# New costs, hand-overs and a table of ranks for the planner of a fused attention and mixture-of-experts kernel

## The chip, the cores and the metric

The kernel runs on one core of a Trainium2 chip. The metric is the time of one execution on the device in microseconds; the time shown is the median of three runs. The core has five engines that each run their own list of instructions in order and hand over by semaphores: PE (matrix products; its weight loads are listed as PEld), DVE, ACT, POOL and SP, which issues the transfers. Operands lie in an on-chip memory of 128 partitions; products accumulate in eight banks beside it.

## The reference

Inputs: `q`, `k`, `v` of shape (8, 8, 576, 64): 8 batches of 8 heads with 576 positions of 64 numbers; `phi` of shape (8, 8, 576, 32); a routing matrix `moe_phi` (512, 32) and the weights `w1` (8, 512, 1024) and `w2` (8, 1024, 512) of 8 experts. All is float32.

```python
def _attn_ref(q, k, v, phi):
    a = softmax(phi over the 576 positions)
    k_m = einsum('bhsm,bhsd->bhmd', a, k)     # 32 pooled keys
    v_m = einsum('bhsm,bhsd->bhmd', a, v)     # 32 pooled values
    attn = softmax(scale * q @ k_m^T over the 32)
    return attn @ v_m

def _moe_ref(x, phi, w1, w2):                 # x: (4608, 512)
    logits = x @ phi                          # (4608, 32 slots)
    d = softmax(logits over the 4608 rows)
    slot_input = d.T @ x                      # 4 slots per expert
    slot_out[e] = relu(slot_input[e] @ w1[e]) @ w2[e]
    c = softmax(logits over the 32 slots)
    return c @ slot_out
```

The softmaxes are shortened here: subtract the maximum, take the exponential, divide by the sum plus 1e-9. The softmax over 4608 rows spans all batches, so no expert can start before the last batch has been routed.

## The kernel before

**Stages.** The 8 batches are worked in four pairs (`bp` 0 to 3, `g` 0 and 1 within a pair). For a batch, `pool_phi` loads `phi` (576 KB), takes its maximum (DVE, line 541, then a transpose and products on PE, lines 549 and 563), subtracts it (POOL, 579), takes the exponential (ACT, 585), and sums by a tree of additions (POOL, 592) and a product with a mask (PE, 602). `pool_kv` loads `k` and `v` (1152 KB each), pools them in three groups of products (PE, 629), scales the sums (ACT, 645 and 652), turns them (PE, 665 and 670), copies them (ACT, 675 to `vT` and 684 to `kd`), and makes products with `moe_phi` (PE, 692) that are copied to `vpb` (ACT, 705). `q` (1152 KB) is loaded into one of two buffers of the tensor `top` and transposed in two halves (DVE, 730). Then, for a pair and each of four chunks `c` of heads: scores (PE, 746), a transpose (DVE, 760), a softmax over the 32 pooled keys (DVE 776, POOL 781, ACT 786, DVE 791 and 800, POOL 804), a transpose back (DVE, 807) and the slot logits (PE, 815). `route` (from `weigh` on, lines 833 to 1032) takes the exponentials of the logits, the products of these with the attention weights (PE, 943), two more groups of products (979 and 987, and 1018), and stores what the pair adds to the slots' input. For the last pair it ends in SIM, the slots' input (DVE, line 1127).

**Experts and output.** From SIM on PE multiplies with `w1` (line 1227) and `w2` (line 1278), 16 tiles of 1 MB each, the last tile of `w2` loaded in four pieces. Then come the slots' sums (1204, 1211), rounding in two parts (1394, 1399), the output products (1408), copies (1461, 1463) and the stores.

**Space.** Nearly all buffers lie in one tensor, `arena`. 20 buffers for weight tiles lie over those of attention; two more weight tiles go where `q` lay. A weight tile can be loaded when the attention buffers below it have been used for the last time. Four of the 20 have nothing below them. Two buffers each serve `phi` and the pairs of `k` and `v`.

**The order.** The class `Plan` writes the order out. Each step is registered by `add(engine, cost, function, reads, writes, ...)`, with a cost in microseconds and a rank. `order` keeps a time for each engine and for the transfers, and repeatedly takes the step that can start first: its inputs are done, plus a lag (0.2 us, 0.25 if the reader is PE, 0 on the same engine), its engine is free and buffers for its results are free. Ties go to the lower rank. A load's start is the time at which the transfers are free; it ends after its bytes at 380 GB/s plus 2 us. The steps are then issued in this order, so every engine runs its part of it as a fixed list, whatever the real times are. SP's list of loads is one of them: a load whose buffer isn't free holds up the loads behind it. Ranks are set by `plan.at(x)`: 1000 x, growing from step to step. Before, they follow a formula in the pair's number, among them `bp - 1.15 + 0.5 * g` for pooling, `bp - 0.45` for the loads of `q`, `bp + 0.25 * c` for chunks and `bp + 1.2` for routing; weights and all that follows have 20. The first nine loads have a fixed order (`FIRST`). Costs come from short formulas for each engine; that for PE is

```python
def pe(n, cols, cnt, passes=2, tiles=1):
    return n * max(0.0185, (cols / 1200.0 + cnt * passes / 2400.0) / tiles)
```

`fill` adds products with a matrix of ones (line 506), 40 of them registered for the start at the lowest rank, and ten around the last pair's routing. Those for the start are left out where the plan's time is past 25 us.

Of the kernel before, what the change touches and what calls it, by code (L numbers as in the profile page):

```python
# [20 lines left out]
class Plan:  # L21
# [7 lines left out]
    LAG = 0.2  # L29
    LAG_PE = 0.25  # L30
# [3 lines left out]
    FILL_END = 25.0  # L34

# [9 lines left out]
    def add(self, eng, cost, fn, r=(), w=(), also=(), pri=None, dma=0.0, slack=0.0):  # L45
        i = len(self.ops)
# [28 lines left out]
        self.ops.append((eng, cost, fn, deps, pri, dma, tiles, need, slack))  # L75

    def order(self):
# [10 lines left out]
        dma_free = 0.0  # L88
        out = []
        while ready:  # L90
# [28 lines left out]
            eng, cost, _, _, pri, dma, tiles, need, _ = ops[i]  # L119
# [13 lines left out]
            for x in tiles:  # L133
                x.users -= 1
                x.end = max(x.end, end[i] + self.LAG)
# [121 lines left out]
def kernel(  # L257
# [174 lines left out]
    WC = 0.45  # L432
# [23 lines left out]
    add(DVE, 1.8, f, r=[ident_b], w=[maskhp_b, maskc_b, rep_b, ones_b])  # L456
# [27 lines left out]
    DMA_RATE = 380e3  # L484

    def load(dst, src, nbytes, w, pri=None):
        add(
            SP, 0.06, lambda: nc.sync.dma_start(dst(), src), w=[w],
            dma=nbytes / DMA_RATE, pri=pri,
        )  # L490


    FIRST = ["phi0", "phi1", "mphi", "q0", "k0", "v0", "q1", "k1", "v1"]
# [30 lines left out]
    add(POOL, 1.0, f, r=[mphi_b], w=[mphd_b])  # L524
# [6 lines left out]
    def pool_phi(b):  # L531
        pt = phis.tile()
        ph = lambda: pt.ap.rearrange("p (c j m) -> p c j m", c=C, j=J)
        load(
            lambda: pt.ap.rearrange("p (c x) -> p c x", c=C), rows(phi, b), H * S * M * 4, pt,
            pri=first(f"phi{b}"),
        )
        mx, mh, mb, es, rs = pmxs.tile(), pmhs.tile(), pmbs.tile(), pess.tile(), prss.tile()
        add(
            DVE, 2.2,  # L540
            lambda: nc.vector.tensor_reduce(  # L541
                mx.ap, ph().rearrange("p c j m -> p c m j"), axis=AX.X, op=ALU.max
            ),
            r=[pt], w=[mx],
        )
        t0 = b_m.tile()
        add(
            PE, TP,
            lambda: nc.tensor.transpose(t0.ap[:, :P], mx.ap.rearrange("p c m -> p (c m)"), ident),
            r=[mx, ident_b], w=[t0], also=[mh],  # L550
        )
        add(
            DVE, dve(P),
            lambda: nc.vector.tensor_reduce(
                mh.ap, t0.ap[:, :P].rearrange("x (a p) -> x a p", a=2), axis=AX.X, op=ALU.max
            ),
            r=[t0], w=[mh],
        )
        t1 = b_m.tile()

        def f():
            for a in range(2):
                nc.tensor.matmul(
                    t1.ap[HALF * a: HALF * a + HALF, :P],
                    mh.ap[:, a: a + 1].to_broadcast([P, HALF]),
                    ident,
                    start=True,
                    stop=True,
                )

        add(PE, pe(4, HALF, P, tiles=2), f, r=[mh, ident_b], w=[t1], also=[mb])
        add(
            ACT, act(128),
            lambda: nc.scalar.copy(mb.ap.rearrange("p c m -> p (c m)"), t1.ap[:, :P]),  # L574
            r=[t1], w=[mb],
        )
        add(
            POOL, pool_tt(PHI_SZ),
            lambda: nc.gpsimd.tensor_tensor(  # L579
                ph(), ph(), mb.ap.unsqueeze(2).to_broadcast([P, C, J, M]), op=ALU.subtract  # L580
            ),
            r=[mb, pt], w=[pt],
        )
        add(
            ACT, act(PHI_SZ, False), lambda: nc.scalar.activation(pt.ap, pt.ap, AF.Exp),  # L585
            r=[pt], w=[pt],
        )
        tr = trees.tile()

        def f():  # L590
            t = tr.ap
            plus = lambda o, x, y: nc.gpsimd.tensor_tensor(o, x, y, op=ALU.add)  # L592
            plus(t, ph()[:, :, 0:4, :], ph()[:, :, 4:8, :])
            plus(t[:, :, 0:2], t[:, :, 0:2], t[:, :, 2:4])
            plus(t[:, :, 0], t[:, :, 0], t[:, :, 1])
            plus(es.ap, t[:, :, 0], ph()[:, :, 8, :])

        add(POOL, pool_tt(512) + pool_tt(256) + 2 * pool_tt(128), f, r=[pt], w=[es, tr])
        sp = b_m.tile()
        add(  # L600
            PE, pe(2, 128, 2),
            lambda: nc.tensor.matmul(
                sp.ap[:, :2], es.ap.rearrange("p c m -> p (c m)"), maskhp, start=True, stop=True
            ),
            r=[es, maskhp_b], w=[sp], also=[rs], slack=S_SLACK,
        )

        def f():
            nc.vector.tensor_scalar(rs.ap, sp.ap[:, :2], EPS, None, op0=ALU.add)
            nc.vector.reciprocal(rs.ap, rs.ap)  # L610

        add(DVE, 0.32, f, r=[sp], w=[rs])
        return pt, ph, rs

    def pool_kv(b, pt, ph, rs, vpb):

        kb = kvs.tile().split(2)
        kv = lambda: kb.ap.rearrange("p (i c x) -> p i c x", i=2, c=C)
        for i, (src, name) in enumerate(((k, "k"), (v, "v"))):
            load(lambda i=i: kv()[:, i], rows(src, b), H * S * D * 4, kb.part(i), pri=first(f"{name}{b}"))  # L620
        acc = b_kv.tile()
        kp, vm = kps.tile(), vms.tile()

        def f(js):
            for j in js:
                for c in range(C):
                    for a in range(2):
                        h0 = HALF * a
                        nc.tensor.matmul(  # L629
                            acc.ap[M * c: M * c + M, a, : 2 * D],  # L630
                            ph()[h0: h0 + HALF, c, j, :],
                            kv()[h0: h0 + HALF, :, c, j * D: j * D + D],
                            start=(j == 0),
                            stop=(j == J - 1),
                            tile_position=(h0, M * c),
                        )

        for js in (range(0, 3), range(3, 6), range(6, 9)):
            add(
                PE, pe(2 * len(js) * H, M, 2 * D, tiles=8), lambda f=f, js=js: f(js),  # L640
                r=[pt, kb], w=[acc], also=[kp, vm],
            )
        def f():
            for a in range(2):
                nc.scalar.activation(
                    kp.ap.rearrange("p i (r x) -> p i r x", r=R)[:, :, :, HALF * a: HALF * a + Y],
                    acc.ap[:, a, :D].rearrange("p (i x) -> p i x", i=2).unsqueeze(2)
                    .to_broadcast([P, 2, R, Y]),
                    AF.Copy, scale=rs.ap[:, a: a + 1],
                )  # L650
            for a in range(2):
                nc.scalar.activation(  # L652
                    vm.ap[:, a], acc.ap[:, a, D: 2 * D], AF.Copy, scale=rs.ap[:, a: a + 1]
                )

        add(ACT, 2 * act(P) + 2 * act(D), f, r=[acc, rs], w=[kp, vm])

        tp, tv = b_m.tile(), b_m.tile()
        kd, vT = kbs.tile(), vTs.tile()

        def f():
            o = tp.ap.rearrange("p (i c r m) -> p i c r m", i=2, c=C, r=R)
            for i in range(2):
                for r in range(R):
                    nc.tensor.transpose(o[:, i, :, r, :], kp.ap[:, i, r * P: r * P + P], ident)

        add(PE, 4 * 0.11, f, r=[kp, ident_b], w=[tp], also=[kd])
        add(
            PE, TP,
            lambda: nc.tensor.transpose(tv.ap[:, :P], vm.ap.rearrange("p a d -> p (a d)"), ident),  # L670
            r=[vm, ident_b], w=[tv], also=[vT],
        )
        add(
            ACT, act(2 * P),
            lambda: nc.scalar.copy(
                vT.ap,
                tv.ap[:, :P].rearrange("p (c m) -> p c m", c=C).unsqueeze(2)
                .to_broadcast([P, C, R, M]),
# [829 lines left out]
```

## Time and profile before

| | |
|---|---|
| median of 3 runs (lowest to highest) | 209.78 us (209.73 to 210.0) |
| the profiled execution | 209.3 us, with a span of 207.5 us |
| mean granted clock of PE | 0.931 |
| busy, of the span: PE, DVE, POOL, ACT | 82%, 64%, 41%, 34% |
| read, written | 66.65 MB, 9.44 MB |
| SIM written, last expert product begun | 145.68 us, 177.34 us |
| waits of SP for PE's pooled products (line 629) | 39.5 us in 7 waits |
| waits of SP for DVE's reciprocal (line 800) | 15.5 us in 3 waits |

The span runs from the first to the last instruction; the time of the execution includes what lies around it. Times in the trace count from the start of the span. A row of a group gives line, engine, operation, result and input, count, then busy time and the mean of one in ns, then the time for which the engine stood idle before it and who ended the wait. "issue" there means that the trace shows nothing that was waited for. The DMA share is the mean busy share of the 16 transfer engines and can come out slightly above 1. A busy PE is not a PE at full speed: its clock is granted in steps, and the column for it is 1.00 at full clock.

### The profile page before, as it was taken

To read this page: it belongs to the slowest core of one execution; us is meant where nothing else is said; L and a number is where in the kernel's file an instruction comes from. 1 tells how busy PE (TensorE), PEld (TensorE's weight loads), DVE (VectorE), ACT (ScalarE), POOL (GpSimd) and SP (SyncE) were. 2 spreads that over 40 slices of the span, in tenths; PEclk is the share of its full clock that TensorE was granted. 3 is DMA by queue.
4 is the path that set the end of the run, shared out by engine and by line. 5 is a ranking of instruction groups with operands and counts; after the bars stand their busy time and mean duration, and the time that the engine had idled before them with its cause. 6 is when DMAs were issued, how large, how long until landed. Compare 5 with 4: busy or idle time off the path is not lost.

```text
span 207.5 us, 5943 instructions
## 1 busy us (share of the span) xinstructions
PE 170.3 (82%) x2571; PEld 109.1 (53%) x2571; DVE 133.3 (64%) x232; ACT 69.8 (34%) x183; POOL 84.4 (41%) x84
## 2 busy tenths in 40 slices
PE   7899777788299899769997979699999999999400
PEld 6577654546176466437566535456556555646100
DVE  7843244969916999995797499547609580387600
ACT  2031425246341661531664233211001331466400
POOL 7199107779690489389793248400000000000000
PEclk9999999969859999996999699999999999999855
DMA  6999999999999999999988999999999998079996
GB/s 207 367 391 393 381 389 381 390 382 384 390 380 392 387 391 406 345 393 390 378 325 288 400 411 417 405 409 407 400 413 405 412 405 302 2 292 410 417 417 287
DMA packets 28986, 76.47 MB, mean 369 GB/s; under 512 B 1824, under 2 KB 6944, under 8 KB 28960
## 3 DMA queue, kind: packets, MB, share of 16 engines
q1 hardware_dynamic: 28960, 76.09, 96.4%
q8 instruction: 20, 0.33, 0.7%
q14 instruction: 6, 0.05, 0.1%
HBM read 66.65 MB, written 9.44 MB: 367 GB/s over the span
## 4 chain that ended last, share of the span: by engine, by line
PE 50%; DVE 16%; DMA 14%; POOL 6%; issue 4%; ACT 2%; SPq 1%; DVEq 1%; POOLq 0%; ACTq 0%
DMA top<-in_q_dram 11%; PE bank L1227 7%; PE bank L815 6%; PE scbank L746 6%; PE kvbank L629 5%; PE kvbank L506 5%; PE kvbank L1278 4%; DMA out_dram<-arena 4%; PE scbank L1278 3%; DVE arena L730 3%; PE bank L1408 3%; PE bank L943 2%; POOL arena L804 2%; DVE arena L760 2%; DVE arena L541 2%
## 5 line engine op out<-in xcount | busy, mean ns | idle before, releaser
L579 POOL TENSOR_TENSOR arena<-arena 128x1152 f32<-128x1152 f32 x8 | 21.0, 2630 | 16.2 <-ACT arena L574 13.6
L506 PE MATMUL kvbank<-ones 128*128 128x256 f32 x88 | 25.2, 421 | 2.2 <-ACT arena L652 1.1
L730 DVE STREAM_TRANSPOSE arena<-top 128x1152 f32<-128x1152 f32 x16 | 21.7, 1360 | 7.2 <-DMA top<-in_q_dram 7.2
L815 PE MATMUL bank<-arena 128*128 128x288 f32 x64 | 21.7, 467 | 4.7 <-DVE arena L807 4.7
L746 PE MATMUL scbank<-arena 64*64 64x288 f32 x256 | 22.0, 442 | 3.0 <-DVE arena L760 2.5
L804 POOL TENSOR_TENSOR arena<-arena,ssm 128x576 f32<-128x576 f32 x16 | 18.3, 1152 | 15.0 <-DVE ssm L800 15.0
L592 POOL TENSOR_TENSOR arena<-arena 128x128 f32<-128x128 f32 (+2 forms) x32 | 23.4, 730 | 2.3 <-ACT arena L585 0.3
L781 POOL TENSOR_TENSOR arena<-arena,smx 128x576 f32<-128x576 f32 x16 | 18.4, 1152 | 13.6 <-DVE smx L776 13.6
L629 PE MATMUL kvbank<-arena 64*32 64x128 f32 x1152 | 21.6, 286 | 2.4 <-issue 1.8
L629 PEld LDWEIGHTS kvbank<-arena 64*32 64x32 f32 x1152 | 17.2, 110 | 6.5 <-issue 4.3
L506 PEld LDWEIGHTS kvbank<-ones 128*128 128x128 f32 x88 | 16.8, 205 | 6.9 <-issue 2.1
L541 DVE TENSOR_REDUCE arena<-arena 128x128 f32<-128x1152 f32 x8 | 17.1, 2142 | 3.9 <-DMA arena<-in_phi_dram 3.9
L760 DVE STREAM_TRANSPOSE arena<-scbank 128x576 f32<-128x576 f32 x16 | 12.2, 764 | 9.3 <-PE scbank L746 9.3
L815 PEld LDWEIGHTS bank<-arena 128*128 128x128 f32 x64 | 12.0, 207 | 10.8 <-DVE arena L807 6.4
L1408 PE MATMUL bank<-sr,cT 64*128 64x512 f32 (+1 forms) x78 | 14.2, 420 | 1.4 <-DVE arena L1463 0.8
L746 PEld LDWEIGHTS scbank<-arena 64*64 64x64 f32 x256 | 9.5, 142 | 11.0 <-DVE arena L760 4.5
L807 DVE STREAM_TRANSPOSE arena<-arena 128x576 f32<-128x576 f32 x16 | 12.2, 760 | 4.0 <-POOL arena L804 3.9
L786 ACT ACTIVATE arena<-arena 128x576 f32<-128x576 f32 x16 | 11.0, 688 | 8.5 <-POOL arena L781 8.5
L1463 DVE COPY arena<-bank 128x512 f32<-128x512 f32 x17 | 11.0, 687 | 3.7 <-DMA out_dram<-arena 2.4
L1227 PE MATMUL bank<-arena,SIM 128*32 128x256 f32 x224 | 12.5, 379 | 0.4 <-DVE SIM L1127 0.4
L1408 PEld LDWEIGHTS bank<-sr,cT 64*128 64x128 f32 x78 | 8.3, 184 | 7.3 <-DVE arena L1463 5.3
L776 DVE TENSOR_REDUCE smx<-arena 128x18 f32<-128x576 f32 x16 | 11.8, 738 | 0.3
(130 smaller groups left out, 242.4 us busy)
## 6 DMA issues: line engine op xcount, KB each, us to landing
arena<-in_moe_w_dram SPq DMA_DIRECT2D x29, 1024.0 KB, 10.1
top<-in_q_dram SPq DMA_DIRECT2D x8, 1152.0 KB, 13.6
arena<-in_k_dram SPq DMA_DIRECT2D x8, 1152.0 KB, 10.7
arena<-in_v_dram SPq DMA_DIRECT2D x8, 1152.0 KB, 13.1
out_dram<-arena SPq DMA_DIRECT2D x11, 768.0 KB, 8.2
arena<-in_phi_dram SPq DMA_DIRECT2D x8, 576.0 KB, 8.1
top<-in_moe_w_dram SPq DMA_DIRECT2D x2, 1024.0 KB, 6.3
arena<-in_moe_w_dram SPq DMA_DIRECT2D x4, 256.0 KB, 14.7
```

The lines of the kernel that those rows point to most:

```text
L506: lambda: nc.tensor.matmul(warm.ap, ones, ones.unsqueeze(1).to_broadcast([P, 2, P]), start=True, stop=True,),
L541: lambda: nc.vector.tensor_reduce(mx.ap, ph().rearrange("p c j m -> p c m j"), axis=AX.X, op=ALU.max),
L579: lambda: nc.gpsimd.tensor_tensor(ph(), ph(), mb.ap.unsqueeze(2).to_broadcast([P, C, J, M]), op=ALU.subtract),
L592: plus = lambda o, x, y: nc.gpsimd.tensor_tensor(o, x, y, op=ALU.add)
L629: nc.tensor.matmul(acc.ap[M * c: M * c + M, a, : 2 * D], ph()[h0: h0 + HALF, c, j, :], kv()[h0: h0 + HALF, :, c, j * D: j * D + D], start= ...
L730: nc.vector.transpose(qT.ap.rearrange("p (i u y) -> p u i y", i=2, y=Y), qt.ap[:, h * QT_SZ: h * QT_SZ + QT_SZ].rearrange("p (u i x) -> p ...
L746: nc.tensor.matmul(scb.ap[HALF * g: HALF * g + HALF, a, :JY], kb[g].ap[h0: h0 + HALF, i, c].rearrange("p r m -> p (r m)"), qT[g][c // 2].a ...
L781: lambda: nc.gpsimd.tensor_tensor(exv(), exv(), bc(mx), op=ALU.subtract),
L804: lambda: nc.gpsimd.tensor_tensor(exv(), exv(), bc(sm), op=ALU.mult),
L815: nc.tensor.matmul(lp.ap[:, :JY], vpb.ap[:, h, :], aT.ap[:, a * JY: (a + 1) * JY], start=(h == 0), stop=(h == H - 1),)
L1227: nc.tensor.matmul(hb.ap[NS * j: NS * j + NS, :256], SIM.ap[:, 2 * i + c, NS * e: NS * e + NS], wv[:, c, 256 * j: 256 * j + 256], start=(e ...
L1408: nc.tensor.matmul(po.ap[:, : x.stop - x.start], cT[bp].ap[y: y + HALF, j // 2 * P: j // 2 * P + P], sr.ap[y: y + HALF, t, x], start=(t == 0),
```

## The change

The planner's model is changed. The lag is now counted by the engine that hands over: 0.25 us for PE, 0.07 for DVE, ACT and POOL, 0 for SP. Transfers start at 2.3 us; attention's inputs are planned at 386 GB/s and weights at 412. For PE each step has a number of instructions, and the plan lets it cross a block of 256 of them no sooner than 6 us after the crossing before. Some costs are replaced by others.

The steps of a batch are regrouped into a class `Batch` with the parts `load_phi`, `shifted`, `load_kv`, `summed`, `pooled`, `turned`, `load_q` and `turn_q`. It could cut a batch into two units (`HALVES`), but that tuple is empty, so all batches have one. The computation and the shapes of instructions are those of before; in `turned` the copy to `kd` is registered ahead of that to `vT`. Each part has a rank of its own, read from a table with a row for the first pair, the two middle pairs and the last pair.

```diff
-    LAG = 0.2
-    LAG_PE = 0.25
+    LAG = (0.25, 0.07, 0.07, 0.07, 0.0)
+    BLOCK, BLOCK_US, FIRST_BLOCK = 256, 6.0, 193
+    DMA_START = 2.3
...
+        cost, ni = cost if isinstance(cost, tuple) else (cost, 4)
...
+            elif eng == PE:
+                for _ in range(ni):
+                    count += 1
+                    if count == self.BLOCK:
+                        count = 0
+                        x = t + cost / 2
+                        late = max(0.0, crossed + self.BLOCK_US - x)
+                        cost += late
+                        crossed = x + late
...
-                        r = max(r, end[d] + (0.0 if same else self.LAG_PE if ops[u][0] == PE else self.LAG))
+                        r = max(r, end[d] + (0.0 if same else self.LAG[ops[d][0]]))
...
-    WC = 0.45
+    WC = 0.49
...
-    add(DVE, 1.8, f, r=[ident_b], w=[maskhp_b, maskc_b, rep_b, ones_b])
+    add(DVE, 3.0, f, r=[ident_b], w=[maskhp_b, maskc_b, rep_b, ones_b])
...
-    DMA_RATE = 380e3
+    DMA_RATE = 412e3
+    IN_RATE = 386e3
...
-    add(POOL, 1.0, f, r=[mphi_b], w=[mphd_b])
+    add(POOL, 3.6, f, r=[mphi_b], w=[mphd_b])
...
-        add(POOL, pool_tt(512) + pool_tt(256) + 2 * pool_tt(128), f, r=[pt], w=[es, tr])
+            add(POOL, 0.5 + 2.66 / self.units, f, r=[pt.part(u)], w=[es.part(u), tr])
...
-                PE, pe(2 * len(js) * H, M, 2 * D, tiles=8), lambda f=f, js=js: f(js),
+                    PE, (0.075 * len(js) * self.ks, 8 * len(js) * self.ks), lambda f=f, js=js: f(js),
...
-        add(PE, 4 * 0.11, f, r=[kp, ident_b], w=[tp], also=[kd])
+            add(PE, (0.5, 8), f, r=[kp.part(u), ident_b], w=[tp], also=[kd])
...
-        add(PE, 0.4, f, r=[vT, mphd_b], w=[vpp], also=[vpb])
+            add(PE, (0.13 * ks, 4 * ks), f, r=[vT.part(u), mphd_b], w=[vpp], also=[vpb])
...
-        add(PE, 1.0, f, r=[qT[0][c // 2], qT[1][c // 2], *kb], w=[scb], also=[ex])
+        add(PE, (1.05, 32), f, r=[*(x.qT[c // 2] for x in pair), *(x.kd.part(x.part(c)) for x in pair)], w=[scb], also=[ex])
...
-        add(PE, 0.96, f, r=[aT, vpb], w=[lp])
+        add(PE, (1.1, 8), f, r=[aT, *(vpb.part(4 * u + x) for x in range(4))], w=[lp])
...
-        add(PE, 1.3 if bp < NSEG - 1 else 1.65, f, r=[df, ex], w=wp, also=[wt])
+        add(PE, (1.6, 72), f, r=[df, ex], w=wp, also=[wt])
...
-        add(PE, 1.3, f, r=[wt, rep_b], w=[wtp], also=[wtb])
+        add(PE, (1.4, 24), f, r=[wt, rep_b], w=[wtp], also=[wtb])
...
-        add(PE, 0.6, f, r=[wtb, *vm], w=[sip])
+        add(PE, (0.5, 16), f, r=[wtb, *(x.vm for x in pair)], w=[sip])
...
+    HALVES = ()
+    AT = (
+        dict(
+            phi=(-1.705, -2.946, -2.863, -1.886), kv=(-0.702, -0.388, -0.807, 0.687),
+            pool=(-1.466, -0.339, -1.36, -1.856), q=(-2.516, -1.841, -2.166, -2.025),
+            turn=(0.504, -0.618), chunk=(0.032, 0.327, 0.478, 0.492),
+            logit=(1.313, -0.355, -1.3, 0.485), route=-0.034,
+        ),
+        dict(
+            phi=(-3.631, -2.992), kv=(-1.771, -2.348), pool=(-0.774, -0.615), q=(0.409, 1.558),
+            turn=(1.059, 0.998), chunk=(0.106, 0.219, 0.401, 0.611),
+            logit=(-2.612, -2.214, -1.572, -0.776), route=1.408,
+        ),
+        dict(
+            phi=(-0.872, -0.956), kv=(-0.757, -0.522), pool=(-1.049, -0.412), q=(-1.042, -1.118),
+            turn=(-0.279, 0.997), chunk=(0.501, 0.524, -0.903, 1.688),
+            logit=(-0.899, 0.078, -1.255, 0.253), route=1.446,
+        ),
+    )
...
-            plan.at(bp - 1.15 + 0.5 * g, 8)
...
-        plan.at(bp - 0.45)
...
-            plan.at(bp - 0.2 + 0.4 * h)
...
-            plan.at(bp + 0.25 * c, 15)
...
-        plan.at(bp + (1.2 if bp < NBP - 1 else 1.0), 10)
+        units = 2 if bp in HALVES else 1
+        vpb = vpbs.tile().split(4 * units)
+        pair = [Batch(2 * bp + g, units) for g in range(2)]
+        at = AT[(bp > 0) + (bp == NBP - 1)]
+        for u in range(units):
+            for x in pair:
+                i = 2 * u + x.g
+                plan.at(bp + at["phi"][i], 8)
+                x.load_phi(u)
+                x.shifted(u)
+                plan.at(bp + at["kv"][i], 8)
+                x.load_kv(u)
+                plan.at(bp + at["pool"][i], 8)
+                x.summed(u)
+                x.pooled(u)
+                x.turned(u, vpb)
+            for x in pair:
+                plan.at(bp + at["q"][2 * u + x.g])
+                x.load_q(u)
+        for h in range(2):
+            plan.at(bp + at["turn"][h])
+            for x in pair:
+                x.turn_q(h)
...
+            plan.at(bp + at["chunk"][c], 15)
             scores(c, pair, ex)
             aT = softmax(c, ex)
+            plan.at(bp + at["logit"][c], 15)
+            logits(c, aT, vpb, pair[0].part(c), lp)
...
+        plan.at(bp + at["route"], 10)
```

A lower number goes first. For the second pair (`bp` = 1), for instance, the load of `phi` of its first batch has rank 1 - 3.631, the load of `q` of its second batch 1 + 1.558.

More of the change, by code (lines that the diff above doesn't have):

```diff
@@ L522, in f @@
             )
-    add(POOL, 1.0, f, r=[mphi_b], w=[mphd_b])
+    add(POOL, 3.6, f, r=[mphi_b], w=[mphd_b])
     def rows(x, b):
         return x[b].rearrange("h (p j) y -> (h p) (j y)", j=J).rearrange("(c r) x -> r c x", r=P)
[L531 to L568, printed above, removed]
-                )
[L571 to L596, printed above, removed]
-        add(POOL, pool_tt(512) + pool_tt(256) + 2 * pool_tt(128), f, r=[pt], w=[es, tr])
[L599 to L613, printed above, removed]
@@ L731, in f, with shifted @@
                     qT.ap.rearrange("p (i u y) -> p u i y", i=2, y=Y),
                     qt.ap[:, h * QT_SZ: h * QT_SZ + QT_SZ].rearrange("p (u i x) -> p u i x", i=2, x=Y),
-                )
-            halves.append((qT, f))
-        return halves
-    def scores(c, qT, kb, ex):
+                ),
+                r=[qt.part(h)], w=[qT],
+            )
+        def shifted(self, u):
+            pt, mx, mb, n = self.pt, self.mx, self.mb, self.n
+            mh = pmhs.tile()
+            c0, c1 = u * self.ks, u * self.ks + self.ks
+            ph = lambda: pt.ap.rearrange("p (c j m) -> p c j m", c=C, j=J)[:, c0:c1]
+            add(
+                DVE, 0.1 + 2.1 / self.units,
+                lambda: nc.vector.tensor_reduce(
+                    mx.ap[:, c0:c1], ph().rearrange("p c j m -> p c m j"), axis=AX.X, op=ALU.max
+                ),
+                r=[pt.part(u)], w=[mx.part(u)],
+            )
+            t0 = b_m.tile()
+            add(
+                PE, (TP, 2),
+                lambda: nc.tensor.transpose(
+                    t0.ap[:n, :P], mx.ap[:, c0:c1].rearrange("p c m -> p (c m)"), ident
+                ),
+                r=[mx.part(u), ident_b], w=[t0], also=[mh],
+            )
+            add(
+                DVE, dve(P),
+                lambda: nc.vector.tensor_reduce(
+                    mh.ap[:n], t0.ap[:n, :P].rearrange("x (a p) -> x a p", a=2), axis=AX.X, op=ALU.max
+                ),
+                r=[t0], w=[mh],
+            )
+            t1 = b_m.tile()
+            def f():
+                for a in range(2):
+                    nc.tensor.matmul(
+                        t1.ap[HALF * a: HALF * a + HALF, :n],
+                        mh.ap[:n, a: a + 1].to_broadcast([n, HALF]),
+                        ident[:n, :n],
+                        start=True,
+                        stop=True,
+                    )
+            add(PE, (pe(4, HALF, n, tiles=2), 8), f, r=[mh, ident_b], w=[t1], also=[mb])
+            add(
+                ACT, act(n),
+                lambda: nc.scalar.copy(
+                    mb.ap[:, c0:c1].rearrange("p c m -> p (c m)"), t1.ap[:, :n]
+                ),
+                r=[t1], w=[mb.part(u)],
+            )
+            add(
+                POOL, pool_tt(PHI_SZ // self.units),
+                lambda: nc.gpsimd.tensor_tensor(
+                    ph(), ph(), mb.ap[:, c0:c1].unsqueeze(2).to_broadcast([P, c1 - c0, J, M]),
+                    op=ALU.subtract,
+                ),
+                r=[mb.part(u), pt.part(u)], w=[pt.part(u)],
+            )
+            ex = lambda: pt.ap.rearrange("p (c x) -> p c x", c=C)[:, c0:c1]
+            add(
+                ACT, act(PHI_SZ // self.units, False),
+                lambda: nc.scalar.activation(ex(), ex(), AF.Exp),
+                r=[pt.part(u)], w=[pt.part(u)],
+            )
@@ L739, in scores @@
+    def scores(c, pair, ex):
         scb = b_s2.tile()
@@ L808, in softmax, with logits @@
         return aT
[L810 removed]
+    def logits(c, aT, vpb, u, lp):
         def f():
@@ new lines @@
+    AT = (
+        dict(
+            phi=(-1.705, -2.946, -2.863, -1.886),
+            kv=(-0.702, -0.388, -0.807, 0.687),
+            pool=(-1.466, -0.339, -1.36, -1.856),
+            q=(-2.516, -1.841, -2.166, -2.025),
+            turn=(0.504, -0.618),
+            chunk=(0.032, 0.327, 0.478, 0.492),
+            logit=(1.313, -0.355, -1.3, 0.485),
+            route=-0.034,
+        ),
+        dict(
+            phi=(-3.631, -2.992),
+            kv=(-1.771, -2.348),
+            pool=(-0.774, -0.615),
+            q=(0.409, 1.558),
+            turn=(1.059, 0.998),
+            chunk=(0.106, 0.219, 0.401, 0.611),
+            logit=(-2.612, -2.214, -1.572, -0.776),
+            route=1.408,
+        ),
+        dict(
+            phi=(-0.872, -0.956),
+            kv=(-0.757, -0.522),
+            pool=(-1.049, -0.412),
+            q=(-1.042, -1.118),
+            turn=(-0.279, 0.997),
+            chunk=(0.501, 0.524, -0.903, 1.688),
+            logit=(-0.899, 0.078, -1.255, 0.253),
+            route=1.446,
+        ),
+    )
@@ L1059 @@
         for c in range(C):
-            plan.at(bp + 0.25 * c, 15)
-            scores(c, qT, kb, ex)
+            plan.at(bp + at["chunk"][c], 15)
+            scores(c, pair, ex)
             aT = softmax(c, ex)
-            logits(c, aT, vpb, lp)
+            plan.at(bp + at["logit"][c], 15)
+            logits(c, aT, vpb, pair[0].part(c), lp)
         if bp < NBP - 1:
@@ L1068 @@
             )
-        plan.at(bp + (1.2 if bp < NBP - 1 else 1.0), 10)
+        plan.at(bp + at["route"], 10)
         if bp == NBP - 1:
             fill(NTAIL, FILL + 1, [MB.part(NSEG - 2)])
-        last = route(bp, ex, vm, lp)
+        last = route(bp, ex, pair, lp)
     plan.at(20)
```

309 lines of the change are left out of this document (179 added, 130 removed).

## The prediction

> **What bounds the kernel now.** First the page of the profile: the busy shares, then the throughput in forty slices of 5.19 us.
>
> ```profile
> span 207.5 us, 5943 instructions
> PE 170.3 (82%) x2571; PEld 109.1 (53%) x2571; DVE 133.3 (64%) x232; ACT 69.8 (34%) x183; POOL 84.4 (41%) x84
> GB/s 207 367 391 393 381 389 381 390 382 384 390 380 392 387 391 406 345 393 390 378 325 288 400 411 417 405 409 407 400 413 405 412 405 302 2 292 410 417 417 287
> q8 instruction: 20, 0.33, 0.7%
> HBM read 66.65 MB, written 9.44 MB: 367 GB/s over the span
> ```
>
> No engine is full, but the transfers run near 390 and later 410 GB/s except in the first slice, around slices 21 and 22 and at the turn from reading to writing. Next the chain of waits, from the end of attention on.
>
> ```profile
> 145.68 0.30 DVE SIM L1127
> 146.03 7.98 PE bank L1227 x144
> ...
> 154.37 6.18 PE bank L1227 x112
> 160.55 0.43 PE kvbank L1278 x8
> ...
> 177.34 0.48 PE kvbank L1278 x8
> 177.84 0.43 DVE cS L1204
> ...
> 188.08 7.27 DMA out_dram<-arena
> ```
>
> Once SIM is written at 146.03, PE multiplies without a pause to 177.84: 31.8 us of expert work. What follows, to the end of the span, is 207.5 - 177.84 = 29.7 us, mostly the writing of the output. So the end is the end of the expert work plus 29.7, and a microsecond won before SIM is worth a microsecond as long as weights have arrived. Whether they have is read from a table of stretches (columns: PE, PEld, DVE, ACT and POOL busy, then granted clock, DMA share, GB/s).
>
> ```profile
> 2.00:10.00 8.00, 7.18 (x29) 5.29 (x28) 6.86 (x12) 0.28 (x2) 2.91 (x6) 1.00 1.04 351
> 10.00:84.00 74.00, 61.57 (x1222) 42.58 (x1220) 49.52 (x73) 28.90 (x73) 48.77 (x44) 0.93 1.06 389
> 84.00:86.00 2.00, 1.34 (x8) 0.74 (x7) 1.90 (x3) 1.77 (x8) 0.36 (x1) 1.00 0.80 282
> ...
> 106.00:108.00 2.00, 2.00 (x42) 0.73 (x25) 2.00 (x4) 0.27 (x2) 1.76 (x4) 1.00 0.84 334
> 108.00:110.00 2.00, 2.00 (x55) 1.35 (x53) 2.00 (x3) 1.09 (x6) 2.00 (x3) 1.00 0.17 63
> ...
> 116.00:170.00 54.00, 49.39 (x628) 28.92 (x630) 35.47 (x81) 12.50 (x40) 9.52 (x9) 0.99 1.02 408
> 170.00:176.50 6.50, 6.50 (x117) 3.77 (x109) 1.23 (x3) 0.80 (x3) 0.00 (x0) 1.00 0.88 314
> ```
>
> Reading ends at about 176.5, only 1.3 us before the last expert product. Two limits therefore end together: PE's expert work counted from SIM, and the bytes. Moving SIM alone wins about 1 us; for more, the transfers must lose less time too. What they lose lies in three rows: against a share of 1.05, the stretch from 84 loses 2 x (1 - 0.80/1.05) = 0.5 us, that from 106 0.4, that from 108 1.7, together **2.6 us**. Why the queue is empty there, from the order of time of SP, DVE and PE:
>
> ```profile
> 98.23 1.39 SPq L488 DMA_DIRECT2D arena<-in_moe_w_dram  x3
> 108.75 0.37 SPq L488 DMA_DIRECT2D top<-in_moe_w_dram  x1
> 109.94 0.88 SPq L488 DMA_DIRECT2D arena<-in_moe_w_dram  x2
> 107.36 1.36 DVE L730 STREAM_TRANSPOSE arena<-top 128x1152 f32<-128x1152 f32 x1
> 108.83 0.94 PE L629 MATMUL kvbank<-arena 64*32 64x128 f32 x48
> ```
>
> Three weight loads of 1 MB issued at 98.23 are used up by 108; the next goes into the q buffer, which the transpose from 107.36 leaves at 108.72, and the two after it into the k/v buffer that the last pooled products leave at 109.77. Space, thus the pace of attention, holds the transfers up.
>
> That pace, last: stretches at half clock, and two of the stretches just before them.
>
> ```profile
> 42.30:45.70 3.40, 3.40 (x25) 1.93 (x25) 2.23 (x5) 1.53 (x6) 2.25 (x3) 0.51 1.05 385
> 56.00:62.60 6.60, 5.71 (x65) 4.28 (x65) 1.75 (x4) 3.06 (x7) 6.20 (x6) 0.50 1.07 384
> 93.80:97.10 3.30, 3.30 (x63) 2.30 (x46) 1.41 (x3) 0.90 (x2) 3.06 (x6) 0.52 1.06 394
> 114.00:117.40 3.40, 3.40 (x20) 2.13 (x21) 1.18 (x2) 0.86 (x2) 1.15 (x1) 0.50 1.00 401
> ...
> 51.90:56.00 4.10, 0.89 (x7) 0.56 (x7) 4.07 (x8) 0.70 (x3) 2.46 (x5) 1.00 1.05 387
> 111.40:114.00 2.60, 1.52 (x12) 1.10 (x12) 2.49 (x6) 1.45 (x7) 0.00 (x0) 1.00 1.04 406
> ```
>
> PE spends 16.7 us at half clock, each time after a stretch in which it stood waiting for a full DVE. The chain of waits runs over PE there: its logits piece takes 2.29 us at half clock, 1.23 at full.
>
> ```profile
> 56.89 2.29 PE bank L815 x4
> ...
> 62.74 1.23 PE bank L815 x4
> ```
>
> **The change part by part.** The instructions stay the same but for some warm-up products: HALVES is empty, so every batch is one unit. All is order. The order is made by a planner that takes the operation that can start first, by its own clock; the engines then run it as written.
>
> *Durations.* The old costs against three pieces of work of this profile, in order of time, beside the logits piece above:
>
> ```profile
> 98.51 1.20 PE L746 MATMUL scbank<-arena 64*64 64x288 f32 x16
> 103.66 0.94 PE L629 MATMUL kvbank<-arena 64*32 64x128 f32 x48
> 105.26 3.16 POOL L592 TENSOR_TENSOR arena<-arena 128x512 f32<-128x512 f32 x4
> ```
>
> The pooled products were planned at 48 x 0.0185 = 0.89 us a third, and are planned at 0.90 now, against 0.94: no news. Scores were 1.0 and become 1.05, against 1.20; logits 0.96 and become 1.1, against 1.23; the sum tree 0.4 + 1024 x 0.0022 = 2.65 and becomes 3.16, as measured. Per pair the old plan was short by 4 x 0.05 + 4 x 0.14 = 0.8 us on PE and by 2 x 0.5 = 1.0 us on POOL against the new one; routing adds 0.3 + 0.1 on PE (1.3 to 1.6, 1.3 to 1.4). So in each pair of some 30 us (four between 26 and 146) PE's plan drifted by about 1.2 us: enough to put an instruction in front of one that was ready, as before 56.89, too little to explain all stalls. The larger lever is the table, which lets pooling, turning, scores, logits and routing of two neighbouring pairs interleave anew. I cannot turn this into an order by hand. Bounds for what attention gains: up to the half-clock loss, 16.7 / 2 = 8.3 us, if no such stretch is left; down to 3.2 us lost, the price of one more idle stretch and its slow window (C below). The 16.7 us are five windows of 3.3; I take two of the five to go, **3.3 us**, which is nearer to the middle of the bounds, 2.6, than to either end.
>
> *Blocks.* The planner now lets PE cross 256 instructions no sooner than 6 us after the last crossing. The page shows 20 instruction packets of 0.33 MB in all, 16 KB each, and there are stops inside a run of ready products with nothing to wait for:
>
> ```profile
> 29.02 0.84 PE L629 MATMUL kvbank<-arena 64*32 64x128 f32 x34 [0.96 <-issue]
> 83.44 0.43 PE L629 MATMUL kvbank<-arena 64*32 64x128 f32 x10 [0.80 <-issue]
> ```
>
> They are not removed by planning; an order that fills them wins at most their 1.8 us, and at least nothing. I count none by itself; it is within the 3.3. [...]
>
> *Hand-overs* fall from 0.2 or 0.25 to 0.07 except behind PE (0.25), and SP's first byte and rates (2.3 us, 386 and 412 GB/s) come close to the 389 and 408 above. These move planned times by tenths and have no price of their own: between -0.3 and +0.3 us, taken as 0.
>
> *Ranks.* They only decide between operations ready together. On SP, loads wait for buffers, so ranks bind little: q's rank behind the next pairs' k and v matters only when both buffers are free. If so, q comes two loads of 1152 KB later, 2 x 1.18 MB / 0.389 = 6 us. q is on the chain now (`top<-in_q_dram`), which is why it returns as a rival. In `turned` the copy to kd goes before the one to vT on ACT: about 0.4 us earlier for scores, 0.6 later for the slot products, both under the PE work of the other batch; if that cover were gone, 0.2 lost per batch, 1.6 at most.
>
> ```profile
> L684 ACT COPY arena<-bank 128x512 f32<-128x512 f32 x8 | 4.7, 587 | 5.8 <-PE bank L665 5.8
> L675 ACT COPY arena<-bank 128x256 f32<-128x256 f32 x8 | 3.0, 376 | 0.8 <-PE bank L670 0.8
> 22.49 14.60 DMA top<-in_q_dram
> ```
>
> **The sum.** Attention 3.3 us faster puts SIM at 142.7 and PE's end at 174.5; the buffers freed as much sooner close the 2.6 us of gaps, so reading ends at 173.9 and the last product, 1.3 later, at 175.2. The later one counts: 177.84 - 175.2 = 2.6 us gained. The profiled execution took 209.3, so 206.7; it ran 0.48 below the median of the runs, 209.78, which makes **207.2**.
>
> How far can it go? Of the 66.65 MB read, 32 loads of 1 MB, 33.55, are weights and 33.1 attention input; at 408 and 389 they take 82.2 + 85.1 us; the stretch from 2 to 10 shows 2.81 MB, an effective start at 2.8; the stretch from 170 shows 2.04 MB in 6.5 us, 1.5 more than at full rate. Together 171.6 against 176.5: at most 4.9 us, **204.9**.
>
> **The rivals.**
>
> *A: bytes at their bound.* Attention gains 5 us or more, and mixed weight loads recover as well: 204.9 to 205.8. For it: in the row from 10 to 84 the DVE is busy 49.5 of 74 us and PE 61.6, so room exists. Against: it needs almost every half-clock stretch gone.
>
> *B: buffers decide anyway.* The empty queue at 108 waits for the last pooled products and the last q transpose; if these come no earlier, only SIM can move, and 1 us of that counts: 208.8 to 209.8. For it: every weight load in that stretch waits for space, whatever its rank. Against: both waits are on attention's own work, which the plan reorders.
>
> *C: PE goes slow in the last pair (slower).* The planner knows no clock. Behind 117.4 the clock is 0.99 and warm-up products fill PE. If the new ranks gather DVE work there as at 51.9, where PE is busy 0.89 of 4.10 us, or q lands late, one slow window of 3.4 us costs 1.7 and the idle stretch ahead of it about 1.5: SIM 3.2 later, PE's end 3.2 later at once, since PE never pauses after SIM: 213.0. It decides as soon as SIM is later than 146.03; with partial gains elsewhere 210.2 to 213. For it: four places show the effect, and nothing in the plan sees it. Against: they came with a plan that had drifted, and the last pair has fewer loads to wait for.
> [...]
>
> **How the numbers follow.** Forecast (206 to 208.6) 0.54, A 0.10, B 0.13, C 0.23. A measurement of this kernel can tell about 0.2% from no change, 0.4 us. Faster by more: the forecast, A and a little of B, 0.66; within: most of B, 0.11; slower: C, 0.23. The range takes A's bound, 204.9, and goes into C to 211.0, leaving out less than 0.15. The likeliest case alone: 206.0 to 208.6.
>
> **What would show it.** Right: SIM before 144; the DMA share under 0.5 in no stretch of 2 us between 80 and 116; reading over by 174.5; half clock less than 16.7 us in total before SIM; L1227 and L1278 again 31.8 us together, or with pauses for weights if the bytes alone bind. Wrong: SIM at or behind 146, above all with half clock behind 117; an L730 waiting several microseconds for q; or a gap as long as now, only elsewhere.

## The result and the profile after

The changed kernel takes **207.38 us** (median of four runs, 206.77 to 208.05) against 209.75 for the kernel before beside it: a ratio of 0.989, 95% interval 0.9854 to 0.9927. Predicted were 207.2. The profiled execution took 207.2 with a span of 205.4.

Line numbers move: the pooled products are now line 703, scores 812, logits 881, SIM 1232, the products with w1 1332, with w2 1383. First the page of the changed kernel, its busy shares and throughput in slices of 5.14 us:

```profile
span 205.4 us, 5935 instructions
PE 167.9 (82%) x2565; PEld 106.1 (52%) x2565; DVE 133.3 (65%) x232; ACT 69.8 (34%) x183; POOL 84.2 (41%) x84
GB/s 204 365 393 392 382 388 383 388 385 383 395 384 388 381 391 390 388 394 401 406 400 412 406 413 408 407 409 407 410 405 406 410 395 183 0 396 409 415 420 201
```

The dips of slices 21 and 22 are gone. The same stretches as before, then the end of reading (columns as in the prediction's tables):

```profile
84.00:86.00 2.00, 0.75 (x30) 0.38 (x33) 2.00 (x2) 1.27 (x2) 0.72 (x2) 1.00 1.05 387
106.00:108.00 2.00, 2.00 (x24) 0.92 (x23) 1.96 (x5) 0.67 (x2) 0.26 (x1) 1.00 0.99 397
108.00:110.00 2.00, 2.00 (x22) 1.27 (x16) 1.97 (x4) 0.27 (x1) 1.48 (x2) 1.00 1.03 416
170.00:172.00 2.00, 0.57 (x12) 0.08 (x4) 0.00 (x0) 0.00 (x0) 0.00 (x0) 1.00 0.63 229
172.00:174.00 2.00, 1.98 (x20) 1.13 (x24) 0.00 (x0) 0.00 (x0) 0.00 (x0) 0.55 0.38 133
174.00:175.70 1.70, 1.70 (x17) 0.51 (x9) 0.42 (x1) 0.00 (x0) 0.00 (x0) 0.53 0.02 6
```

The chain of waits of the changed kernel from SIM on:

```profile
136.35 0.30 DVE SIM L1232
136.70 7.98 PE bank L1332 x144
...
153.11 18.86 DMA arena<-in_moe_w_dram
172.02 0.96 PE kvbank L1383 x8
172.98 0.85 PE scbank L1383 x8
173.83 0.85 PE kvbank L1383 x8
174.69 1.08 PE scbank L1383 x8
```

SIM comes 9.3 us earlier, but the expert work ends only 2.1 us earlier, at 175.7 instead of 177.8. PE now waits for weights: the chain goes back through a load, and the last four groups of products run at half clock, 0.85 to 1.08 us each for the 0.43 to 0.48 of before. Half clock before SIM is down from 16.7 us in four stretches to 6.9 in two:

```profile
32.30:35.70 3.40, 3.40 (x23) 2.03 (x21) 0.00 (x0) 1.39 (x5) 2.62 (x1) 0.51 1.05 381
56.10:59.60 3.50, 3.50 (x56) 1.83 (x62) 3.38 (x5) 1.74 (x3) 3.50 (x4) 0.51 1.06 380
```

Attention thus gained far more than needed, and the bytes took over as the limit. The experiments ask two things: is that so, and which part of the change made it.

### The profile page after: what moved, and what is told of

It reads as the page before. It is cut to its first block, busy times and chain, and to the rows that moved or that the text cites. A ratio compares the mean times of both kernels' runs of the same rounds, so it can differ in the third digit from the quotient of the medians.

```text
span 205.4 us, 5935 instructions
## 1 busy us (share of the span) xinstructions
PE 167.9 (82%) x2565; PEld 106.1 (52%) x2565; DVE 133.3 (65%) x232; ACT 69.8 (34%) x183; POOL 84.2 (41%) x84
## 4 chain that ended last, share of the span: by engine, by line
PE 37%; DMA 21%; DVE 14%; POOL 11%; issue 4%; SPq 4%; ACT 2%; POOLq 1%; DVEq 1%; ACTq 0%
DMA arena<-in_moe_w_dram 9%; DMA arena<-in_v_dram 8%; PE bank L1332 7%; PE scbank L812 6%; PE kvbank L703 4%; PE bank L881 4%; SPq L501 4%; DMA out_dram<-arena 4%; POOL arena L847 3%; POOL arena L668 3%; PE bank L1513 3%; POOL arena L647 3%; POOL arena L870 2%; PE bank L1009 2%; DVE arena L605 2%
## 5 line engine op out<-in xcount | busy, mean ns | idle before, releaser
L703 PE MATMUL kvbank<-arena 64*32 64x128 f32 x1152 | 21.0, 277 | 6.2 <-issue 2.7
L812 PE MATMUL scbank<-arena 64*64 64x288 f32 x256 | 23.7, 447 | 2.3 <-DVE arena L826 2.3
L519 PE MATMUL kvbank<-ones 128*128 128x256 f32 x82 | 23.4, 422 | 2.4 <-ACT arena L727 1.3
L703 PEld LDWEIGHTS kvbank<-arena 64*32 64x32 f32 x1152 | 16.5, 107 | 10.8 <-issue 5.6
L881 PE MATMUL bank<-arena 128*128 128x288 f32 x64 | 18.7, 425 | 1.3 <-DVE arena L873 0.8
L519 PEld LDWEIGHTS kvbank<-ones 128*128 128x128 f32 x82 | 15.8, 207 | 6.0 <-ACT arena L727 1.7
L1513 PE MATMUL bank<-sr,cT 64*128 64x512 f32 (+1 forms) x78 | 14.7, 425 | 1.7 <-DVE arena L1568 1.3
L881 PEld LDWEIGHTS bank<-arena 128*128 128x128 f32 x64 | 11.2, 189 | 6.4 <-DVE arena L873 2.1
L1383 PE MATMUL kvbank<-arena 128*32 128x256 f32 x128 | 10.8, 411 | 3.8 <-DMA arena<-in_moe_w_dram 3.8
L857 DVE TENSOR_REDUCE ssm<-arena 128x18 f32<-128x576 f32 x16 | 11.8, 738 | 1.0 <-ACT arena L852 0.7
```

Of the source, the lines that this page charges most:

```text
L519: lambda: nc.tensor.matmul(warm.ap, ones, ones.unsqueeze(1).to_broadcast([P, 2, P]), start=True, stop=True,),
L703: nc.tensor.matmul(acc.ap[M * c: M * c + M, a, : 2 * D], ph()[h0: h0 + HALF, c, j, :], kv()[h0: h0 + HALF, :, c, j * D: j * D + D], start= ...
L812: nc.tensor.matmul(scb.ap[HALF * g: HALF * g + HALF, a, :JY], pair[g].kd.ap[h0: h0 + HALF, i, c].rearrange("p r m -> p (r m)"), pair[g].qT ...
L881: nc.tensor.matmul(lp.ap[:, :JY], vpb.ap[:, h, :], aT.ap[:, a * JY: (a + 1) * JY], start=(h == 0), stop=(h == H - 1),)
L1513: nc.tensor.matmul(po.ap[:, : x.stop - x.start], cT[bp].ap[y: y + HALF, j // 2 * P: j // 2 * P + P], sr.ap[y: y + HALF, t, x], start=(t == 0),
```

## The experiments

Three sets of four, each set on one chip beside the kernel before, whose medians there were 209.65, 209.41 and 209.12 us. Between sets the ratios compare, not the times.

### SIM delayed: does PE's chain still bind?

```diff
-        nc.vector.tensor_mul(SIT.ap, part, bc(rst.ap[:, 1]))
+        for _ in range(21):
+            nc.vector.tensor_mul(SIT.ap, part, bc(rst.ap[:, 1]))
```

> The changed kernel with one product ahead of SIM done 21 times instead of once (the same result; 20 x 0.28 = 5.6 us more on DVE), in the same order of instructions. Theory: bytes bind, PE's work behind SIM has slack. SIM at 142.3 plus 31.8 is 174.1, no later than the 175.7 at which PE ends now, so the time stays at 207.4, or falls by up to 1.5 us since PE no longer stops for weights and its clock stays up. Rival: PE's chain from SIM on still sets the end, and the time grows by 5.6 us to 213.

Measured: 210.45 us, ratio 1.0038 (1.0006 to 1.0069), between the two expectations. The delay carried a second cost along. In this run's table of stretches PE stands idle beside the repeated work and goes to half clock, and its chain shows the price:

```profile
139.00:149.00 10.00, 5.61 (x56) 2.63 (x60) 6.58 (x17) 0.00 (x0) 0.00 (x0) 0.50 0.91 350
```

```profile
143.04 0.30 DVE SIM L1233
143.39 10.74 PE bank L1333 x144
```

10.74 us for the products that take 7.98 at full clock. The space that these free came later too: up to 160 us SP waits 11 times for products with w1, 23.0 us in all, and the share falls to 0.91. So the run didn't answer the question, and it was repeated with PE kept busy:

```diff
                         start=(g == 0),
                         stop=(g == 1),
                     )
+            for _ in range(12 if bp == NSEG - 1 else 0):
+                nc.tensor.matmul(warm.ap, ones, ones.unsqueeze(1).to_broadcast([P, 2, P]), start=True, stop=True)
```

The twelve products stand in the last step of `route`, behind its own products for the last pair.

> The changed kernel with SIM 6.5 us later by repeated work on DVE as before, and twelve products of ones (5.2 us) on PE beside it. In the run without these PE stood still and its clock fell to 0.50 from 140 to 149, so that the first 16 tiles of w1 took 2.8 us more. Theory (bytes bind): SIM at 143.0 plus 31.8 us is 174.8, within 0.9 of where PE ends in the changed kernel, 175.7: 206 to 207.6. Rival (PE's chain from SIM on binds): 213.

Measured: 206.74 us, ratio 0.9902 (0.987 to 0.9935), the same as the changed kernel's 0.989. The chain of this run:

```profile
143.08 0.30 DVE SIM L1238
143.43 7.98 PE bank L1338 x144
...
151.78 6.18 PE bank L1338 x112
...
175.41 0.48 PE kvbank L1389 x8
```

SIM 6.7 us later costs nothing measurable. PE's chain from SIM on therefore doesn't set the end of the changed kernel; some 7 of the 9.3 us won in attention are slack. They are about all the slack there is: the delayed kernel no longer waits for a load and ends its expert work at 175.89, the changed kernel at 175.77. That it is the bytes that bind the changed kernel is read from its waits for loads (in all, times, longest, in us):

```profile
PE kvbank L1383 <- DMA arena<-in_moe_w_dram: 3.8, 3, 1.5
```

### Keeping PE's clock up at the end

In `expert_out`, products of ones behind the tiles 12, 13 and 14 of w2, in stretches where PE waits (1, 3 and 4 of them; in a second version 1, 2 and 1):

```diff
+                nw = {12: 1, 13: 3, 14: 4}.get(2 * e + i, 0)
...
+                        for _ in range(nw if d else 0):
+                            nc.tensor.matmul(warm.ap, ones, ones.unsqueeze(1).to_broadcast([P, 2, P]), start=True, stop=True)
```

> The changed kernel with 1, 3 and 4 products of ones (about 0.43 us each) put behind the third, second and last tile but one of w2, in stretches in which PE waits for weights. Theory: the four last groups take 0.85 us instead of 0.43 since PE had waited and its clock fell to 0.50; with the clock held they take 0.43, 1.7 us less, and the sums behind them a little less: 205.5. Rival: what ends the reading (172.0) and the thin transfers behind 170 set the end whatever the clock: 207.2 to 207.6, the groups then waiting for weights one by one.

> As the run with 1, 3 and 4 products of ones behind tiles of w2, but with 1, 2 and 1. There the clock stayed at 1.00, but the last four products of ones, 1.92 us, ran to 175.34 while the last pieces of w2 were there at about 174. Theory: PE's last expert product ends at about 175.0 instead of 176.05, and the time is 205.7 to 206.3. Rival: the last pieces land only at 175, the time stays at 206.7 to 207.1.

Measured: 206.86 us, ratio 0.9859 (0.9825 to 0.9892), and 206.64, ratio 0.9889 (0.9857 to 0.9921). Neither can be told from the changed kernel's 0.989. With 1, 3 and 4 of them the clock did stay at 1.00. In the order of time of the second version the last groups are as expected, but the very last takes 1.23 us for the 0.64 of the one before, which fits a wait for its pieces:

```profile
173.18 0.70 PE L1403 MATMUL kvbank<-ones 128*128 128x256 f32 x2
173.81 0.64 PE L1383 MATMUL kvbank<-arena 128*32 128x256 f32 x8
174.26 1.23 PE L1383 MATMUL scbank<-arena 128*32 128x256 f32 x8
175.42 1.25 PE L1316 MATMUL bank<-cS,rep 128*128 128x256 f32 x4
```

The sums start at 175.42, against 175.69 without. The half clock in the changed kernel's tail looked like a loss of 1.7 us and was worth 0.3, since the last bytes come between 174 and 175 in either case (a share of 0.03 and of 0.04 there). What holds these back? One guess was the pieces of the last tile, with their rows of 1 KB; so the tile was loaded as one load of 1 MB:

```diff
-            last = e == E - 1 and i == 1
+            last = False
```

> The changed kernel with 1, 2 and 1 products of ones as before, and the last tile of w2 loaded as one load of 1 MB instead of four of 256 KB in rows of 1 KB. With the pieces the transfers' share falls to 0.69, 0.56, 0.53 and 0.22 from 170 to 174, and the time was 206.6. If the small rows are why the end is thin, reading ends about 1 us earlier, the last expert products at 174.8 instead of 175.4, and the time is 205.6 to 206.4. If the 16 transfer engines simply finish at different times, both products of the tile wait for its slowest engine, until 174.5, and the time is 206.6 to 207.4.

Measured: 206.76 us, ratio 0.9869 (0.9824 to 0.9914): no difference. In its trace the share of the transfers falls in the same way, 0.96, 0.63, 0.42, 0.18 for the four stretches of 1 us from 170, and the last tile's first product starts at 174.63. So the size of the pieces isn't the reason. That the 16 transfer engines finish at different times fits the falling mean, but no run shows the single engines; it stays open.

### Which part made it: ranks or model

The table with the model of before, and the model with the formula ranks of before; what is left out of the two diffs goes back to the costs and rates of before, and to the ranks of before:

```diff
-    LAG = (0.25, 0.07, 0.07, 0.07, 0.0)
+    LAG = 0.2
+    LAG_PE = 0.25
-    BLOCK, BLOCK_US, FIRST_BLOCK = 256, 6.0, 193
-    DMA_START = 2.3
+    BLOCK, BLOCK_US, FIRST_BLOCK = 256, 0.0, 193
+    DMA_START = 0.0
...
```

```diff
-                plan.at(bp + at["phi"][i], 8)
+                plan.at(bp - 1.15 + 0.5 * x.g, 8)
...
```

> The table of ranks as changed, but the planner's costs, lags, rates and start of before, and no block term. The kernel before ran 209.8 us, the changed one 207.4, with SIM at 136.7 instead of 146.0 and no empty stretch of the queue at 108. If the ranks carry the gain, SIM comes by 140, the queue has no empty stretch, and the time is 207 to 208. If table and model only work together (the rival: the ranks decide ties, and the ties are made by the costs), SIM comes between 142 and 148 and the time is 208.5 to 211.

> The changed costs, lags, rates and blocks, with the formula ranks of before. If the durations carry the gain, SIM comes by 140 and the time is 207 to 208. If the ranks do, or only both together, SIM comes at 143 to 147 and the time is 208.5 to 210.5, near the 209.8 of before: per pair the old plan was short by only 0.8 us on PE and 1.0 us on POOL.

Measured: the table alone 211.84 us, ratio 1.0083 (1.0042 to 1.0125), slower than before; the model alone 209.76, ratio 0.999 (0.9956 to 1.0025), no difference. Neither half wins anything. The table alone did bring SIM early in its profile, and lost it again behind:

```profile
138.29 0.30 DVE SIM L1233
138.64 7.98 PE bank L1333 x144
...
173.63 1.08 PE kvbank L1384 x8
174.71 0.85 PE scbank L1384 x8
175.57 0.90 PE kvbank L1384 x8
...
176.97 1.22 PE bank L1317 x2
178.19 1.06 PE scbank L1384 x8
```

and in its table of stretches:

```profile
170.80:188.00 17.20, 15.23 (x84) 8.57 (x84) 4.79 (x9) 4.68 (x11) 0.00 (x0) 0.51 0.37 133
```

Half clock lasts from 170.8 into the output. Was that all? The same products of ones (1, 2, 1) were added:

> The table with the model of before, plus the same 1, 2 and 1 products of ones. Without them it ran 211.8 us although SIM came at 138.6: PE waited for weights, and its clock was at 0.50 from 170.8 on, through the last expert products and into the output. Theory: that is where its gain went; with the clock held the last expert product ends 2 to 3 us earlier and the output runs at full clock: 207 to 208.5. Rival: the old model's order of the tail is the cause, not the clock: 210.5 or more.

Measured: 210.5 us, ratio 1.0033 (1.0 to 1.0066). By the medians that is half a per cent better, but the intervals overlap, and it is not near 0.989. The rival's 210.5 is what came. So the clock in the tail may be a part of the loss, but not all of it. The chain above holds a sign of the rival: the last group of products, at 178.19, stands behind a part of the slots' sums (line 1317); in the changed kernel all groups come before the sums. The trace without the products of ones shows a further loss, a queue that isn't full in attention:

```profile
79.00:82.00 3.00, 1.82 (x53) 1.01 (x49) 2.95 (x7) 1.78 (x7) 1.15 (x1) 0.99 0.59 194
```

How the loss is shared between these isn't shown: the trace of the run with products of ones is of an execution of 212.4 us and doesn't explain the median. The table needs the new model.

### The block term, and how exact the model must be

```diff
-    BLOCK, BLOCK_US, FIRST_BLOCK = 256, 6.0, 193
+    BLOCK, BLOCK_US, FIRST_BLOCK = 256, 0.0, 193
```

> The changed kernel planned without the term for blocks of 256 PE instructions, all else as changed. The changed kernel still stops inside ready products (2.67 us at 27.9, 0.25 at 100.7). If planning around the blocks is part of the gain, SIM comes 1 to 4 us later than 136.7 and the time is 207.4 to 209. If it is not, the order differs a little and the time stays within 0.6 of 207.4.

Measured: 211.13 us, ratio 1.0102 (1.0064 to 1.0139): slower than before, by more than either expectation. SIM came at 143.1, as in the delayed kernel, which with that SIM ran at 0.9902. What differs is again the queue, in four stretches of its table:

```profile
42.00:44.00 2.00, 0.66 (x3) 0.38 (x3) 1.96 (x4) 0.68 (x1) 1.14 (x2) 1.00 0.71 197
54.00:56.00 2.00, 1.10 (x6) 0.79 (x5) 1.67 (x6) 0.48 (x3) 1.75 (x1) 1.00 0.78 214
97.00:100.00 3.00, 3.00 (x113) 2.14 (x115) 2.35 (x6) 0.83 (x2) 2.67 (x3) 1.00 0.69 204
111.00:112.00 1.00, 1.00 (x6) 0.78 (x6) 0.87 (x3) 0.65 (x2) 0.50 (x1) 1.00 0.54 217
```

After this the gain looked like that of one lucky order, which any change of the model would lose. Two small changes test that, and a third asks which row of the table matters (None stands for the formula ranks):

```diff
-    LAG = (0.25, 0.07, 0.07, 0.07, 0.0)
+    LAG = (0.26, 0.07, 0.07, 0.07, 0.0)
```

```diff
-    BLOCK, BLOCK_US, FIRST_BLOCK = 256, 6.0, 193
+    BLOCK, BLOCK_US, FIRST_BLOCK = 256, 5.8, 193
```

```diff
-        at = AT[(bp > 0) + (bp == NBP - 1)]
+        at = AT[1] if 0 < bp < NBP - 1 else None
```

> The changed kernel planned with 0.26 instead of 0.25 us for hand-overs from PE; the order changes in a few places of PE, DVE, ACT and SP's loads. Theory: the gain belongs to one order, in which few idle stretches of PE coincide with a slow clock; the model without blocks, the table with the old model, and the new model with the old ranks each gave another order and 209.8 to 211.8. A hundredth of a microsecond then already costs: 208 to 211. Rival: the block term itself is what helps, and an order planned with it stays near 207.4: 207 to 208.

> The changed kernel planned with 5.8 instead of 6.0 us between crossings of blocks of 256 PE instructions. If planning around blocks is what helps, 5.8 does nearly what 6.0 does: 207 to 208. If the gain belongs to one order, the time lies anywhere from 207.5 to 211, with the half-clock time before SIM between 7 and 17 us as its measure.

> The changed model; the table's row for the middle pairs alone, formula ranks for the first and last pair. With formula ranks throughout it ran 209.8, SIM at 147. The gaps of the queue that the table closed lie in the middle and third pair (84 to 86, 106 to 110). If its middle row does it, SIM comes by 141 and the time is 207 to 208.5; if the rows work only together, 209 to 211.

Measured: 207.14 us, ratio 0.988 (0.9832 to 0.9929); 207.43, ratio 0.9901 (0.9867 to 0.9936); 207.42, ratio 0.9893 (0.9848 to 0.9939). All three keep the whole gain. How far their orders differ can be counted in the lists that the planner writes. Against the changed kernel, another step stands in 5 of PE's 264 places with 5.8 us, in 14 with the longer lag and in 61 with the middle row alone; for SP it is 0, 2 and 12 of 82 places. The first two are close neighbours, and the third is clearly another order. So the theory of the one lucky order falls. The row for the middle pairs, with the new model, carries the gain by itself; the rows for the first and last pair add nothing measurable. The lag run shows more. It has a slow stretch in the last pair:

```profile
123.80:130.70 6.90, 6.35 (x15) 4.05 (x14) 2.15 (x4) 0.22 (x1) 2.09 (x2) 0.52 1.03 408
```

SIM comes at 140.2 there, 3.9 us behind the changed kernel's, and the time is the same: slack again. What the kernels at ratio 0.99 share is a full queue. Worked out from stretches of 1 us between 10 and 168 of one execution each (what the DMA share lacks to 1.03, as a part of 1.03, summed), the lost time is 0.9 us in the changed kernel, 1.0, 1.0 and 1.4 in these three, against 3.8 before, 3.9 without the block term and 2.2 for the table alone. The sum doesn't tell everything: the last two kernels are slower than the one before, though they lose hardly more time in it, or less. For the table alone the tail adds to it; for the run without the block term the rest of the difference isn't accounted for.

Open is how the block term does it, and even whether it does: only one order without it was run (another step in 75 of PE's 264 places and in 21 of SP's 82), and that one may be a bad order for other reasons. PE's stop in it behind the same 699 records took 2.84 us against 2.67, hardly longer; what its order does worse is the queue. Nor was it taken apart which of the costs, lags and rates the table needs.

## Why the prediction was right

*The two limits, right.* PE's chain from SIM and the bytes ended together before, and the prediction let the later one count. This decided the number: the delayed SIM shows that the chain no longer counts, and the waits for loads what does.

*The last tenths, in part luck.* The profiled execution was put at 206.7 and took 207.2, as the expert work ended at 175.77 and not at 175.2. The forecast of the median added 0.48 us, the distance in the kernel before; here it was 0.18. The errors of 0.5 and 0.3 pull against each other, which is why 207.2 stands so close to 207.38.

*The gaps of the queue, right in place and size.* 2.6 us were to close; the lost time fell from 3.8 to 0.9, 2.9 by the sum over stretches. The sum put the end of the last product at 175.2; it was 175.77. The rest went at the end of reading, where the transfers run thin.

*Attention's gain, mis-sized.* The term was 3.3 us, two of five slow windows; measured are 9.3. Three of the five are gone (6.9 us at half clock for 16.7), and the engines wait less for each other: in the 18 us from 42 DVE is busy 17.18 us instead of 13.84, PE 14.80 instead of 13.04. The upper bound of 8.3, half the slow time, was no bound, because waiting is not slow work. This error cost nothing, since beyond some 3 us nothing before SIM counts. Rival A named that condition, attention 5 us faster, but put the time at 204.9 to 205.8; its floor took the thin end of reading from before, 1.5 us beyond full rate. In the changed kernel the three stretches from 170 move 0.73 MB until about 174.4, 2.6 us more than at 408 GB/s.

*Durations and table, half right.* The durations alone were called too little, and they are (0.999). The table was called the larger lever; alone it makes the kernel slower (1.0083). That the two only work together was not foreseen.

*Blocks, wrong.* The prediction gave that term no price of its own. In the one order planned without it the ratio is 1.0102, with it 0.989; that it is the term and not just that order isn't shown.

*Ranks on SP, right.* q didn't come late. The only long wait for it is at the start, 7.49 us against 6.19 before, and none follows:

```profile
18.99 1.38 DVE L590 STREAM_TRANSPOSE arena<-top 128x1152 f32<-128x1152 f32 x1 [7.49 <-DMA top<-in_q_dram]
```

The two copies in `turned` show little: PE's weight loads wait 1.1 us for the copy to `kd` and 1.8 us for that to `vT`, against 0.7 and 0.3 before.

*Rival B, wrong:* the last pooled products came at 102.9 instead of 108.8, the last q transpose at 109.9 instead of 113.7. *Rival C, right in its mechanism and wrong in its price:* the lag run has just that slow stretch in the last pair, 6.9 us at a clock of 0.52 behind the 4 us from 120, in which DVE is busy 3.99 us and PE 1.82; and it is free. Its point of decision, SIM later than 146.03, was out of reach: PE starts on SIM at 140.51 there, and even the delayed kernel's 143.43 cost nothing.

## What to carry to other kernels

When two limits end together, price a change by the one it moves less; beyond that, what it wins is slack, and a delay put in on purpose, with the engine's clock held up, shows how much. A planner's ranks and its model are one thing: a table that wins under one model can lose under another, so test them together and apart before either gets the credit. A visible loss, such as products at half clock, is worth only what the next limit behind it leaves.

## What the runs showed of the hardware that was not expected

PE's stops within ready products lie multiples of 256 of its instructions apart, two in each of two kernels: 2.67 and 0.25 us in the changed kernel, 0.96 and 0.80 us in the one before. The rows of a table from 0 up to a stop count PE's and PEld's records. Of the changed kernel and of the kernel before:

```profile
0.00:30.55 30.55, 23.57 (x349) 18.42 (x350) 15.78 (x23) 6.76 (x13) 15.31 (x22) 1.00 0.98 354
0.00:100.90 100.90, 85.48 (x1622) 58.31 (x1623) 75.47 (x115) 40.90 (x103) 71.42 (x73) 0.97 1.03 379
```

```profile
0.00:29.00 29.00, 24.78 (x349) 19.27 (x349) 15.11 (x23) 6.76 (x13) 15.30 (x22) 1.00 0.99 352
0.00:83.42 83.42, 69.15 (x1239) 48.40 (x1239) 56.80 (x85) 29.99 (x74) 52.99 (x56) 0.94 1.03 376
```

699 and 3245 records, 698 and 2478. The traces list semaphore instructions and one drain on PE besides, 6 and 20 up to these stops, 7 and 19 in the kernel before. With them the counts are 705 and 3265, 705 and 2497, which is 2560 = 10 x 256 and 1792 = 7 x 256 apart: all are 193 + 256 k, the planner's count, with k = 2 and 12, 2 and 9. Most such places show no stop of this kind: of the thirteen that the changed kernel passes up to 100.9 us, these two do. With the table and the old model, PE's busy time stands still from 63.5 to 65.77, 2.27 us, behind 1974 records, where 193 + 256 k is 1985 for k = 7. What PE waited for there isn't shown:

```profile
0.00:63.50 63.50, 53.20 (x987) 37.65 (x987) 43.22 (x62) 22.32 (x52) 42.05 (x46) 1.00 1.03 371
0.00:65.77 65.77, 53.21 (x987) 37.65 (x987) 43.64 (x63) 22.56 (x52) 42.05 (x46) 1.00 1.03 371
```

The clock: without the twelve products of ones, PE is busy 5.61 of the 10 us from 139 in the delayed kernel and its clock is 0.50; with them it is busy 8.29 us and the clock is 1.00. The twelve products took the delayed kernel from a ratio of 1.0038 to 0.9902, about 2.8 us of 209.5, as much as the 10.74 - 7.98 = 2.76 us that the first products with w1 lose at half clock.
